# Linear attention and an MLP under one planned order: weight scales from sums of squares, dependencies by up to eight ranges, other virtual times

## The chip, the cores and the metric

The kernel runs on one core of one Trainium2 chip. The core has a matrix engine (PE, with its weight loads listed apart as PEld), a vector engine (DVE), a scalar engine (ACT), a general engine (POOL) and queues that issue DMAs (SP above all). Each engine works through its own instructions in order, and waits where one needs a result of another. The metric is the time of one execution in microseconds. For the kernel before it is the median of three runs.

## The reference

Inputs are `q`, `k`, `v` of shape (8, 8, 576, 64), a projection `w_phi` (64 x 128) and the weights of an MLP, `w_in` (512 x 2048) and `w_out` (2048 x 512). Batch, heads, rows and head width are B, H, S and D.

```python
def phi(x):
    proj = np.einsum('bhsd,df->bhsf', x, w_phi)
    proj = proj - np.max(np.abs(proj), axis=-1, keepdims=True)
    return np.concatenate([np.exp(proj), np.exp(-proj)], axis=-1)
q_p, k_p = (phi(q), phi(k))
kv = np.einsum('bhsf,bhsd->bhfd', k_p, v)
z = np.sum(k_p, axis=2)
num = np.einsum('bhsf,bhfd->bhsd', q_p, kv)
den = np.einsum('bhsf,bhf->bhs', q_p, z)[..., None] + 1e-06
x = (num / den).transpose(0, 2, 1, 3).reshape(B * S, H * D)   # 4608 x 512
h = x @ w_in
out = (h * (1.0 / (1.0 + np.exp(-1.702 * h)))) @ w_out
```

The two weight matrices of the MLP arrive as 8-byte floats: one 128 x 512 block is 512 KB in the profile's list of transfers. The kernel reads their bits as 64-bit integers.

## The kernel before, in words

**Work.** `attention(b)` turns one batch into `x16`, 16-bit high and low parts of the MLP's input, with 512 features on 4 x 128 partitions and the 576 rows of the batch as columns (tile `x`, shape 128 x 2 x 4 x 576). It goes head pair by head pair (`attn_unit`, four to a batch): 512 rows of a pair fill columns 0:512 of one of the four feature groups. The last 64 rows of all heads are done together (`attn_tail`), and `attn_last` (L1086) writes them, when the last pair is through, into columns 512:576 of all 2 x 4 groups at once. The first five units are computed in fp32 (`exact`), the others in split 16-bit pieces.

`moe_chunk` (L1128) does the MLP for a strip of 256 or 384 rows of `x`. For each of 16 blocks `j` of 128 hidden units, 12 matmuls (four feature groups, three products of high and low parts) fill a hidden tile in PSUM (`hps`, two buffers `hb`). ACT takes a tanh (`th`), DVE multiplies (`g`), ACT and DVE split the result in 16-bit parts (`gh`, `gl`), and three matmuls for each 128 rows add it to an output tile (`acc`, three buffers `ab`). The first 512 rows go through the first eight blocks, then through the other eight (`part_` 0 and 1, each in two strips of 256), with the first half's sums kept; the rest of the rows take all 16 blocks in one go.

**Weights.** `load_weights(j)` (L518) reads two blocks of 128 x 512 8-byte floats, one of each matrix, into a staging place: a spare `x` tile (three buffers) or the still unused end of `wbuf`. POOL, ACT and two DVE operations make an fp32 block of each, with the 32-bit words `lo` and `hi` of the raw data as strided views. The first of the two DVE operations leaves magnitudes in place of the `lo` words. Their upper halves, read as bf16, are the moving operand of four matmuls whose stationary operand is a 9-column slice of `pick`, a matrix of zeros with one column of ones. So `wsum` collects, per column of a block, sums of absolute values over the partitions; for `w_in` each block has a row of its own. `weight_scales(k)` (L588) takes the maxima of a half, rounds them down to powers of two and spreads them over the partitions with a matmul; out come `wg`, `sw`, `pg` and, after the second half, `al`. `split_weights(j)` (L609) then scales a block and splits it into 16-bit high and low parts: one operation on ACT, one on DVE. It writes over the block ahead of its source, so the operation on ACT for one block has to wait until DVE has read the block before.

**Order.** The whole order is planned before any instruction is emitted. Each operation is recorded (`Recorder.record`) with a modelled cost and with what it depends on: `touch` (L189) compares the regions that operations read and write in a tile. A region (`V.region`, L77) is a range of partitions and one range of bytes, from the first element to the last; what a strided view leaves out in between counts as touched. `schedule` (L274) goes through the engines like a list scheduler. It takes what could start first, and among what is ready the smaller priority. Operations of a part with `first` for their engine come ahead of all others there. After that goes a virtual time, which `R.part(v0, v1, first)` gives to a stretch of the program. One unit is a chunk of 384 rows of the MLP, whose first strip starts at 0, so that the set-up has negative times. `emit` writes the operations in the planned order. The waits between engines are put in afterwards, from the accesses of the emitted instructions and not from the recorded regions.

The virtual times are at the end of the function (L1183 on): `v_att` for the attention units, `VB` for how long ahead of a batch the maxima of `v` are taken, `WV` for the weights of the two halves (start, step per block, scales) and `SV` for their splits (offset, length). The MLP has first place on DVE and ACT; the split of the first half has it too.

Almost all instructions have one line in the profile, L390, where the recorder emits them. They are told apart by their tiles: `hb<-x,wbuf` is the first product of the MLP, `ab<-wbuf,gh` and `ab<-wbuf,gl` the second, `hb<-...,pick` and `ab<-...,pick` the sums of the weights, `at<-ii,zt` the transposition in `attn_last`, and `wbuf<-wbuf,sw` the splits.

Of the kernel before, what the change touches and what calls it, by code (L numbers as in the profile page):

```python
# [10 lines left out]
F16 = mybir.dt.float16  # L11
BF16 = mybir.dt.bfloat16
I32 = mybir.dt.int32
U32 = mybir.dt.uint32
I64 = mybir.dt.int64
AF = mybir.ActivationFunctionType
# [4 lines left out]
P = 128  # L21
# [25 lines left out]
class V:  # L47
# [29 lines left out]
    def region(self):  # L77
        ap = self.t
        pat = ap.ap
        row = pat[0][0]  # L80
        p0 = ap.start_partition()
        if self.tl.whole:
            return (p0, p0 + pat[0][1], 0, 1 << 20)
# [29 lines left out]
class Recorder:  # L113
# [75 lines left out]
    def touch(self, o, a, write):  # L189
        tl = a.tl  # L190
        self.claim(o, tl)
        p0, p1, b0, b1 = a.region()
        keep = []
        for ent in tl.log:
            (q0, q1, c0, c1), w, d = ent
# [3 lines left out]
            if not (write and d is not o and p0 <= q0 and q1 <= p1 and b0 <= c0 and c1 <= b1):  # L199
                keep.append(ent)  # L200
        keep.append(((p0, p1, b0, b1), write, o))
        tl.log = keep

    @staticmethod
# [189 lines left out]
def attn_moe_kernel(ctx, tc, q, k, v, w_phi, w_in, w_out, out):  # L394
# [12 lines left out]
    NH = 2  # L407
# [59 lines left out]
    nc.vector.tensor_copy(ii[0:D], ident[0:D, 0:D])  # L467
    nc.vector.tensor_copy(ii[D:P], ident[D:P, D:P])

    ones = cp.tile([16, P], F32, name="ones")  # L470
    nc.gpsimd.memset(ones, 1.0)

    wst = static("wst", [P, NF], F32)
    wb = static("wb", [P, 2 * NF], F32)
# [34 lines left out]
        )  # L509
        R.vector.tensor_scalar(dst, dst, 2.0**-50, None, ALU.max)  # L510


    NS = NJ // NH + 1
    pick = cp.tile([P, 2 * NS - 1], BF16, name="pick")
    nc.gpsimd.memset(pick, 0.0)
    nc.gpsimd.memset(pick[:, NS - 1 : NS], 1.0)

    def load_weights(j, wsum, first, last):  # L518
        js = slice(j * P, (j + 1) * P)
        stage = None  # L520
        if WIDE and (j % 4 > 1 or j >= NJ - 4):
            stage = new("x").rearrange("p a c s -> p (a c s)")
        for i, src in (
            (2 * j, w_in[:, js].rearrange("(c p) f -> p c f", p=P)),
            (2 * j + 1, w_out[js, :]),
        ):
            dst = wbuf[:, i + 1]
            if not WIDE:
                if i % 2 == 0:
                    dst = dst.rearrange("p (c f) -> p c f", c=NCT)  # L530
                R.sync.dma_start(dst, src)
                z = new("osb")
                R.scalar.activation(z, wbuf[:, i + 1], AF.Abs)
# [54 lines left out]
    def weight_scales(k, wsum):  # L588

        m = small(1, "sc")[0:NS]  # L590
        m2 = small(NS, "sc")[0:NS]
# [638 lines left out]
    for part_ in range(NH):  # L1230
        js = range(part_ * NJ // NH, (part_ + 1) * NJ // NH)
        v0, dv, v1 = WV[part_]
        wsum = R.tile(ab if part_ else hb, whole=True)[0:NS, 0:P]
        for i, j in enumerate(js):
            R.part(v0 + dv * i, v0 + dv * (i + 1))
            load_weights(j, wsum, j == js[0], j == js[-1])
        R.part(v1, v1)
        weight_scales(part_, wsum)
# [59 lines left out]
```

## Time and profile before

| what | value |
|---|---|
| median of 3 runs | 1095.7 us (1092.83 to 1096.32) |
| the profiled execution | 1094.31 us, of which its span is 1092.5 us |
| mean granted clock of PE | 0.993 |
| PE matmuls | 8941 |
| DMA | 88.59 MB, 81 GB/s on average |

The page lists busy time per engine, and the queries behind it give windows of the span, groups of instructions and the timeline of one engine. A line of the timeline has a start, a duration, the engine, the operation, what it writes and reads (out<-in) and how many of them run on; in brackets stands how long the engine was idle before, and what ended that. The duration of a run of matmuls includes the tail of the last one, so the distance between two starts is the better measure of what a run costs. In a window, the pair of numbers for an engine is its busy time and its count of instructions; PEclk is the share of full clock granted to PE.

### The profile page before, as it was taken

The page shows a single profiled execution, that of the slowest core. Times are in us where ns is not written, and L with a number is a line of the kernel's source. Part 1 is how long each engine was busy: PE and PEld are TensorE (multiplying, and loading weights), DVE is VectorE, ACT ScalarE, POOL GpSimd, SP SyncE. Part 2 cuts the span into 40 slices and gives each one's busy share as a digit, 9 for nine tenths or more (in the row PEclk, how much of TensorE's full clock was granted, in tenths as well). Part 3 has the DMA queues.
Part 4 walks back from the last instruction along what each step waited for, and adds up shares of the span by engine and source line. Part 5 has one row for each costly group of instructions (what it writes and reads, how often), then busy time and mean ns, then how long its engine had stood idle before and what let it go on. Part 6 is the DMA issues. An engine that isn't in the chain of part 4 may idle for free.

```text
span 1092.5 us, 22970 instructions
## 1 busy us (share of the span) xinstructions
PE 1055.1 (97%) x8941; PEld 728.4 (67%) x8941; DVE 866.8 (79%) x1802; ACT 713.4 (65%) x1488; POOL 249.8 (23%) x322
## 2 busy tenths in 40 slices
PE   5996999999999999999999999999999999999997
PEld 3664677668876666578866666678776666577653
DVE  5999999999999997898789987898779766332323
ACT  4677687678787676686667666786567766442422
POOL 6476211241232211301122112111123111100000
PEclk9998999999999999999999999999999999999999
DMA  8853342543253441332234442332224220000101
GB/s 274 271 187 123 94 107 64 107 93 89 59 103 92 117 100 42 69 102 59 49 98 92 118 77 55 68 79 59 59 59 78 36 53 11 11 30 1 30 1 29
DMA packets 177452, 88.59 MB, mean 81 GB/s; under 512 B 143424, under 2 KB 168128, under 8 KB 177088
## 3 DMA queue, kind: packets, MB, share of 16 engines
q1 hardware_dynamic: 177184, 86.87, 32.8%
q8 instruction: 70, 1.15, 0.4%
q10 hardware_dynamic: 160, 0.26, 0.1%
q14 instruction: 38, 0.31, 0.1%
HBM read 54.59 MB, written 9.44 MB: 59 GB/s over the span
## 4 chain that ended last, share of the span: by engine, by line
PE 74%; DVE 14%; ACT 5%; DMA 3%; issue 2%; SPq 1%; POOL 1%; DVEq 0%; ACTq 0%
PE ab L390 29%; PE hb L390 28%; PE at L390 17%; DVE sm L390 2%; DMA xT<-xs 2%; DVE t L390 1%; ACT e L390 1%; DVE gl L390 1%; DVE wbuf L390 1%; DVE g L390 1%; DVE ks L390 1%; SPq L390 1%; DMA tl<-in_v_dram 1%; ACT eh L390 1%; DVE xs L390 1%
## 5 line engine op out<-in xcount | busy, mean ns | idle before, releaser
L390 PE MATMUL hb<-x,wbuf 128*128 128x192 f16 (+3 forms) x3264 | 474.5, 280 | 1.0 <-DVE g L390 0.9
L390 PE MATMUL ab<-wbuf,gh 128*128 128x512 f16 x1152 | 337.0, 380 | 2.2 <-ACT gh L390 2.1
L390 PEld LDWEIGHTS <-wbuf 128*128 128x128 f16 x3264 | 277.4, 98 | 79.2 <-issue 2.2
L390 ACT ACTIVATE th<-hb,usc 128x384 f32<-128x384 f32 (+1 forms) x208 | 116.6, 561 | 130.9 <-PE hb L390 120.0
L390 PE MATMUL ab<-wbuf,gl 128*128 128x512 f16 x576 | 193.1, 380 | 2.6 <-DVE gl L390 2.3
L390 DVE SCALAR_TENSOR_TENSOR g<-th,hb 128x384 f32<-128x384 f32 (+1 forms) x208 | 107.3, 516 | 89.7 <-ACT th L390 87.7
L390 PEld LDWEIGHTS <-gh 128*128 128x128 f16 x1152 | 107.7, 98 | 81.7 <-ACT gh L390 5.8
L390 ACT ACTIVATE gh<-g,al 128x384 f16<-128x384 f32 (+1 forms) x176 | 107.8, 613 | 54.4 <-DVE g L390 53.3
L390 DVE SCALAR_TENSOR_TENSOR gl<-g,al,gh 128x384 f16<-128x384 f32 (+1 forms) x176 | 110.0, 625 | 37.3 <-ACT gh L390 30.2
L390 POOL TENSOR_TENSOR xf<-nf,rc 128x512 f32<-128x512 f32 x28 | 32.7, 1169 | 422.6 <-DVE rc L390 376.2
L390 PE MATMUL at<-ph,xT 128*128 128x128 f16 x976 | 107.1, 219 | 0.1
L390 DVE TENSOR_REDUCE sm<-at 128x4 f32<-128x512 f32 x126 | 85.8, 681 | 19.1 <-PE at L390 18.9
L390 ACT ACTIVATE e<-t 128x512 f32<-128x512 f32 x144 | 89.8, 637 | 10.7 <-DVE t L390 10.5
L390 ACT ACTIVATE e<-at 128x512 f32<-128x512 f32 x144 | 85.9, 604 | 14.8 <-PE at L390 12.7
L390 DVE SCALAR_TENSOR_TENSOR t<-at,ks,sm 128x512 f32<-128x512 f32 x122 | 90.4, 743 | 1.1
L390 PEld LDWEIGHTS <-gl 128*128 128x128 f16 x576 | 54.7, 98 | 52.0 <-DVE gl L390 9.6
L390 PE MATMUL at<-vs,eh 128*128 128x132 f32 x216 | 82.5, 383 | 0.0
L390 DVE TENSOR_TENSOR el<-e,eh 128x512 f16<-128x512 f32 x108 | 74.5, 690 | 9.7 <-ACT eh L390 7.9
L390 DVE TENSOR_TENSOR elb<-e,eh 128x512 bf16<-128x512 f32 x110 | 76.7, 698 | 5.9 <-ACT eh L390 4.9
L390 PE MATMUL at<-kzs,eh 128*128 128x132 f32 x224 | 80.3, 373 | 0.0
L390 PEld LDWEIGHTS <-xT 128*128 128x128 f16 x976 | 70.6, 98 | 14.1 <-issue 0.5
L390 ACT ACTIVATE eh<-t 128x512 fp32r<-128x512 f32 x109 | 69.2, 647 | 0.4 <-DVE t L390 0.3
(204 smaller groups left out, 1898.7 us busy)
## 6 DMA issues: line engine op xcount, KB each, us to landing
vn<-in_v_dram SPq DMA_DIRECT2D x64, 128.0 KB, 2.8
kq<-in_k_dram SPq DMA_DIRECT2D x32, 256.0 KB, 3.1
kq<-in_q_dram SPq DMA_DIRECT2D x32, 256.0 KB, 3.0
tl<-in_v_dram SPq DMA_DIRECT2D x18, 384.0 KB, 3.2
x<-in_moe_w_in_dram SPq DMA_DIRECT2D x10, 512.0 KB, 3.9
x<-in_moe_w_out_dram SPq DMA_DIRECT2D x10, 512.0 KB, 4.6
out_dram<-osb SPq DMA_DIRECT2D x36, 128.0 KB, 2.4
out_dram<-osb SPq DMA_DIRECT2D x16, 256.0 KB, 2.6
```

The lines of the kernel that those rows point to most:

```text
L390: f(*[g(a) for a in args], **{k: g(a) for k, a in kw.items()})
```

## The change

It has three parts.

**Ranges.** `region` returns up to eight byte ranges where a view has that many pieces, each at least 32 elements apart from the next; `touch` compares all ranges of both.

```diff
-        lo = ap.offset - p0 * row
-        hi = lo + 1 + sum(s * (n - 1) for s, n in pat[1:])
-        return (p0, p0 + pat[0][1], lo * b, hi * b)
+        los, rest = [ap.offset - p0 * row], list(pat[1:])
+        while rest and len(los) * rest[0][1] <= 8:
+            inner = 1 + sum(s * (n - 1) for s, n in rest[1:])
+            if rest[0][0] < inner + 32:
+                break
+            los = [x + rest[0][0] * k for x in los for k in range(rest[0][1])]
+            rest = rest[1:]
+        n = 1 + sum(s * (n - 1) for s, n in rest)
+        return (p0, p0 + pat[0][1], tuple((x * b, (x + n) * b) for x in los))
...
-            hit = q0 < p1 and p0 < q1 and c0 < b1 and b0 < c1
+            hit = q0 < p1 and p0 < q1 and any(c0 < b1 and b0 < c1 for b0, b1 in rs for c0, c1 in cs)
```

**Sums of squares.** The stationary operand of the weights' matmuls is now the block's own 128 columns, the same as the moving one, so each adds a 128 x 128 product of the block with itself, whose diagonal holds the sums of squares. `w_in` and `w_out` have one such square each in `wsq`. The operands are the upper halves of the finished fp32 weights in `wbuf`, no longer of words in the staging tile. ACT is recorded ahead of POOL. `weight_scales` takes the maxima of both squares, transposes them, takes the maxima again, halves the exponent with an integer shift (a square root, rounded to a power of two) and spreads the two results with a second matmul.

```diff
-                R.gpsimd.tensor_scalar(y, hi.bitcast(F32), 2.0**-112, None, ALU.mult)
-                z = lo
-                R.scalar.activation(z, lo.bitcast(U32), AF.Copy, scale=0.9375 * 2.0**-29)
+                R.scalar.activation(lo, lo.bitcast(U32), AF.Copy, scale=0.9375 * 2.0**-29)
+                R.gpsimd.tensor_scalar(y, hi.bitcast(F32), 2.0**-112, None, ALU.mult)
                 R.vector.scalar_tensor_tensor(
-                    z, y.bitcast(I32), 3, z, ALU.logical_shift_left, ALU.bitwise_or
+                    y.bitcast(I32), y.bitcast(I32), 3, lo, ALU.logical_shift_left, ALU.bitwise_or
                 )
                 R.vector.scalar_tensor_tensor(
-                    dst.bitcast(I32), hi, -(2**31), z, ALU.bitwise_and, ALU.bitwise_or
+                    y.bitcast(I32), hi, -(2**31), y.bitcast(I32), ALU.bitwise_and, ALU.bitwise_or
                 )
-                z = raw.bitcast(BF16).rearrange("p (n w) -> p n w", w=4)[:, :, 1]
-            r = NS - 1 if i % 2 else j % (NS - 1)
+            z = wbuf[:, i + 1].bitcast(BF16).rearrange("p (n w) -> p n w", w=2)[:, :, 1]
             for c in range(NCT):
+                zc = z[:, c * P : (c + 1) * P]
                 R.tensor.matmul(
-                    wsum,
-                    pick[:, NS - 1 - r : 2 * NS - 1 - r],
-                    z[:, c * P : (c + 1) * P],
+                    wsq[:, i % 2],
+                    zc,
+                    zc,
...
-        R.vector.tensor_reduce(m, wsum, AX.X, ALU.max)
-        pow2(m, m)
-        R.vector.tensor_scalar(m2, ident[0:NS, 0:NS], m, None, ALU.mult)
+        R.vector.tensor_reduce(m, wsq, AX.X, ALU.max)
         tp = psa()
-        R.tensor.matmul(tp[:, 0:NS], ones[0:NS], m2, start=True, stop=True)
-        R.vector.tensor_reduce(wg[:, k, 0:1], tp[:, 0 : NS - 1], AX.X, ALU.max)
-        R.vector.tensor_copy(wg[:, k, 1:2], tp[:, NS - 1 : NS])
+        R.tensor.transpose(tp[0:2, 0:P], m, ident)
+        R.vector.tensor_reduce(m1, tp[0:2, 0:P], AX.X, ALU.max)
+        R.vector.tensor_scalar(
+            m1.bitcast(I32), m1.bitcast(I32), 1, 0x7F800000,
+            ALU.logical_shift_right, ALU.bitwise_and,
+        )
+        R.vector.tensor_scalar(m1, m1, 2.0**64, 2.0**-50, ALU.mult, ALU.max)
+        R.vector.tensor_scalar(m2, wone, m1, None, ALU.mult)
+        R.tensor.matmul(tp[:, P : P + 2], ones[0:2], m2, start=True, stop=True)
+        R.vector.tensor_copy(wg[:, k], tp[:, P : P + 2])
```

**Virtual times.** First place on DVE and ACT goes from the split of the first half to that of the second.

```diff
-    VB = 0.532
-    V1 = (-1.793, 0.5)
-    WV = ((-9.335, 0.3, -7.2), (-7.049, 0.246, -5.399))
-    SV = ((-0.438, 1.101), (0.0, 0.212))
+    VB = 0.882
+    V1 = (-1.39, 0.435)
+    WV = ((-9.335, 0.3, -7.395), (-6.76, 0.267, -5.253))
+    SV = ((-0.955, 1.101), (0.223, 0.212))
...
-            return -10.175 + 1.0 * i
+            return -10.175 + 0.983 * i
...
-        return 0.776 + (i - 8) * 0.362
+        return 0.519 + (i - 8) * 0.366
...
-                R.part(u, u + (0.321 if b else 0.1))
+                R.part(u, u + (0.266 if b else 0.1))
...
-            R.part(w, w + (0.537 if b else 0.2))
+            R.part(w, w + (0.517 if b else 0.2))
...
-        R.part(v2, v2 + SV[part_][1], () if part_ else ("vector", "scalar"))
+        R.part(v2, v2 + SV[part_][1], ("vector", "scalar") if part_ else ())
```

More of the change, by code (lines that the diff above doesn't have):

```diff
@@ L13 @@
 I32 = mybir.dt.int32
+I16 = mybir.dt.int16
 U32 = mybir.dt.uint32
@@ L191, in touch @@
         self.claim(o, tl)
-        p0, p1, b0, b1 = a.region()
+        p0, p1, rs = a.region()
         keep = []
         for ent in tl.log:
-            (q0, q1, c0, c1), w, d = ent
-            hit = q0 < p1 and p0 < q1 and c0 < b1 and b0 < c1
+            (q0, q1, cs), w, d = ent
+            hit = q0 < p1 and p0 < q1 and any(c0 < b1 and b0 < c1 for b0, b1 in rs for c0, c1 in cs)
             if hit and (w or write) and d is not o:
                 o.deps[d] = True
-            if not (write and d is not o and p0 <= q0 and q1 <= p1 and b0 <= c0 and c1 <= b1):
+            over = write and d is not o and p0 <= q0 and q1 <= p1
+            if not (over and all(any(b0 <= c0 and c1 <= b1 for b0, b1 in rs) for c0, c1 in cs)):
                 keep.append(ent)
-        keep.append(((p0, p1, b0, b1), write, o))
+        keep.append(((p0, p1, rs), write, o))
         tl.log = keep
@@ L468, in attn_moe_kernel @@
     nc.vector.tensor_copy(ii[D:P], ident[D:P, D:P])
-    ones = cp.tile([16, P], F32, name="ones")
+    ones = cp.tile([2, P], F32, name="ones")
     nc.gpsimd.memset(ones, 1.0)
+    wone = cp.tile([2, 2], F32, name="wone")
+    nc.vector.tensor_scalar(wone[:, 0:1], ident[0:2, 0:1], 16.0, None, ALU.mult)
+    nc.vector.tensor_copy(wone[:, 1:2], ident[0:2, 1:2])
     wst = static("wst", [P, NF], F32)
@@ L510, in pow2, with load_weights @@
         R.vector.tensor_scalar(dst, dst, 2.0**-50, None, ALU.max)
[L513 to L518, printed above, removed]
+    def load_weights(j, wsq, first, last):
         js = slice(j * P, (j + 1) * P)
@@ L531, in load_weights @@
                 R.sync.dma_start(dst, src)
-                z = new("osb")
-                R.scalar.activation(z, wbuf[:, i + 1], AF.Abs)
             else:
@@ L586, in allmax, with weight_scales @@
         R.vector.tensor_copy(dst, tp[:, P : P + 1])
-    def weight_scales(k, wsum):
-        m = small(1, "sc")[0:NS]
-        m2 = small(NS, "sc")[0:NS]
-        R.vector.tensor_reduce(m, wsum, AX.X, ALU.max)
-        pow2(m, m)
-        R.vector.tensor_scalar(m2, ident[0:NS, 0:NS], m, None, ALU.mult)
-        tp = psa()
-        R.tensor.matmul(tp[:, 0:NS], ones[0:NS], m2, start=True, stop=True)
-        R.vector.tensor_reduce(wg[:, k, 0:1], tp[:, 0 : NS - 1], AX.X, ALU.max)
-        R.vector.tensor_copy(wg[:, k, 1:2], tp[:, NS - 1 : NS])
+    def weight_scales(k, wsq):
+        m = small(2, "sc")
+        m1 = small(1, "sc")[0:2]
+        m2 = small(2, "sc")[0:2]
+        R.vector.tensor_reduce(m, wsq, AX.X, ALU.max)
+        tp = psa()
+        R.tensor.transpose(tp[0:2, 0:P], m, ident)
[8 more added lines that the diff above has]
+        R.vector.tensor_copy(wg[:, k], tp[:, P : P + 2])
         R.vector.reciprocal(sw[:, k], wg[:, k])
@@ L1232, in attn_moe_kernel @@
         v0, dv, v1 = WV[part_]
-        wsum = R.tile(ab if part_ else hb, whole=True)[0:NS, 0:P]
+        wsq = R.tile(ab if part_ else hb, whole=True)[:, 0 : 2 * P]
+        wsq = wsq.rearrange("p (t f) -> p t f", t=2)
         for i, j in enumerate(js):
             R.part(v0 + dv * i, v0 + dv * (i + 1))
-            load_weights(j, wsum, j == js[0], j == js[-1])
+            load_weights(j, wsq, j == js[0], j == js[-1])
         R.part(v1, v1)
-        weight_scales(part_, wsum)
+        weight_scales(part_, wsq)
         v2 = v1 + SV[part_][0]
-        R.part(v2, v2 + SV[part_][1], () if part_ else ("vector", "scalar"))
+        R.part(v2, v2 + SV[part_][1], ("vector", "scalar") if part_ else ())
         for j in js:
```

2 lines of the change are left out of this document (1 added, 1 removed).

## The prediction

> **What bounds the kernel now.** I read the page's totals first, then the busy time of each engine by windows, then the timeline of PE where PE is idle.
>
> ```profile
> span 1092.5 us, 22970 instructions
> PE 1055.1 (97%) x8941; PEld 728.4 (67%) x8941; DVE 866.8 (79%) x1802; ACT 713.4 (65%) x1488; POOL 249.8 (23%) x322
> ...
> 50.00:100.00 50.00, 46.41 (x276) 30.29 (x276) 48.18 (x98) 38.81 (x78) 33.38 (x23) 1.00 0.53 167
> 100.00:150.00 50.00, 42.80 (x280) 28.36 (x281) 47.09 (x94) 34.87 (x70) 18.18 (x16) 0.86 0.36 95
> 150.00:200.00 50.00, 49.07 (x474) 37.55 (x472) 49.40 (x106) 42.40 (x96) 10.99 (x13) 1.00 0.36 86
> 200.00:250.00 50.00, 47.91 (x484) 35.64 (x483) 49.43 (x120) 33.45 (x77) 13.50 (x17) 1.00 0.51 110
> 250.00:300.00 50.00, 49.61 (x639) 40.88 (x636) 49.62 (x120) 40.06 (x92) 9.38 (x14) 1.00 0.27 61
> ```
>
> The columns are span, then busy time of PE, weight loads, DVE, ACT and POOL, then PE's granted clock. PE is busy for 1055.1 of 1092.5 us, so it sets the time: only its idle time, its slow clock and its own work can be saved. From 150 to 300 it is idle for at most 2.1 us in 50. Between 100 and 150 it is idle for 7.2 us, and the clock is 0.86. DVE meanwhile is 94 to 99% busy all the way to 300, which the rivals below come back to. The hole itself, in PE's timeline:
>
> ```profile
> 89.19 0.27 PE L390 MATMUL hb<-x,wbuf 128*128 128x256 f16 x1
> ...
> 97.63 0.23 PE L390 MATMUL at<-kzb,eqtlb 128*128 128x132 bf16 x1
> 100.74 1.09 PE L390 MATMUL at<-ident,xf 128*128 128x128 f32 x4 [2.88 <-DVE xf L390]
> 102.44 0.62 PE L390 MATMUL ab<-x,pick 128*9 128x128 bf16 x4 [0.62 <-DVE x L390]
> 105.39 0.62 PE L390 MATMUL ab<-x,pick 128*9 128x128 bf16 x4 [2.32 <-DVE x L390]
> 106.24 0.40 PE L390 MATMUL at<-ii,zt 128*128 128x64 f16 x4 [0.23 <-ACT zt L390]
> 108.12 0.62 PE L390 MATMUL ab<-x,pick 128*9 128x128 bf16 x4 [1.48 <-DVE x L390]
> ...
> 110.84 0.62 PE L390 MATMUL ab<-x,pick 128*9 128x128 bf16 x4 [1.77 <-DVE x L390]
> 111.40 4.75 PE L390 MATMUL hb<-x,wbuf 128*128 128x256 f16 x31
> 115.99 1.03 PE L390 MATMUL ab<-wbuf,gh 128*128 128x512 f16 x4
> ```
>
> From 97.86 to 111.40 PE does a few small groups and waits 2.88 + 0.62 + 2.32 + 0.23 + 1.48 + 1.77 = **9.30 us**. Then the MLP (`hb<-x,wbuf`) breaks loose with 31 matmuls. One matmul of it stands alone at 89.19, and one more of the next hidden tile a little later. They say why it waits. The first matmul of a hidden tile reads columns 0:256 of row 0 of `x`; the second reads row 0 of the low half. `attn_last` writes only columns 512:576 of all eight rows, but L77 records that write as one range from the first to the last byte. Row 0's first 256 columns lie ahead of that range, everything after lies in it. There are two `hb` buffers, so two hidden tiles each issue one matmul and then stand behind `attn_last` in the planned order:
>
> ```profile
> 102.31 0.57 ACT L390 CAST x<-at 128x512 f16<-128x512 f32 x1
> 109.81 0.57 ACT L390 CAST x<-at 128x512 f16<-128x512 f32 x1
> ...
> 104.06 0.68 DVE L390 TENSOR_TENSOR x<-at,x 128x512 f16<-128x512 f32 x1
> ```
>
> What the MLP's first 512 columns need is the last head pair's `x`, complete at 104.06 + 0.68 = 104.74. `attn_last`'s copy ends only at 110.38.
>
> **The change, part by part.** *(a) Ranges.* With up to eight ranges the write becomes its eight true pieces, and the planner may start the MLP at 104.74. The price of one such matmul at full clock comes from a long run:
>
> ```profile
> 149.93 3.45 PE L390 MATMUL hb<-x,wbuf 128*128 128x256 f16 x29
> 153.26 1.04 PE L390 MATMUL ab<-wbuf,gh 128*128 128x512 f16 x4
> ```
>
> That is 3.33 / 29 = 0.115 us. Three of the four row groups of `x` are there earlier, so 9 of 12 matmuls of two hidden tiles, less the two that run already, fit into the wait: 16 x 0.115 = 1.8 us. What stood between 104.74 and 111.40 (three `pick` groups at 0.62 and two groups of `ii,zt` at 0.40, 2.66 us as shown) comes later, at 1.5 us by the prices of (c). Gain: 6.66 - 1.5 + 1.8 = **7.0**. Idle time left before 104.74: 6.88 - 1.09 - 0.2 - 1.8 = 3.8. Bounds: nothing (second rival) to the whole 9.3.
>
> *(b) Clock.* The burst at 111.40 takes 4.59 / 31 = 0.148 us each against 0.115: 1.0 us lost. With 3.8 us still idle I take half, **0.5** (0 to 1.0).
>
> *(c) Sums on PE.* 128 matmuls in 32 groups of four turn from a 9-column to a 128-column stationary operand; `pick` is no longer loaded.
>
> ```profile
> 119.97 0.62 PE L390 MATMUL ab<-x,pick 128*9 128x128 bf16 x4
> 120.52 0.50 PE L390 MATMUL hb<-x,wbuf 128*128 128x256 f16 x3
> 120.86 0.67 PE L390 MATMUL at<-ph,xT 128*128 128x128 f16 x9
> 121.36 0.61 PE L390 MATMUL at<-ident,kq 128*128 128x128 f32 x4
> ...
> 124.25 0.62 PE L390 MATMUL ab<-x,pick 128*9 128x128 bf16 x4
> ...
> L390 PEld LDWEIGHTS <-xT 128*128 128x128 f16 x976 | 70.6, 98 | 14.1 <-issue 0.5
> L390 PEld LDWEIGHTS at<-kzs,eh 128*128 128x128 f32 x224 | 42.6, 191 | 2.9 <-issue 0.5 <-POOL vt L390 0.4 <-POOL kzs L390 0.3
> L390 PEld LDWEIGHTS <-pick 128*9 128x9 bf16 x128 | 11.4, 99 | 12.8 <-issue 11.2 <-DMA wbuf<-in_moe_w_out_dram 0.2
> ```
>
> A `pick` group holds PE for 0.55 us. Nine full-width matmuls of 128 columns go in 0.50, so four take 0.22: 0.33 saved per group. The last of the 32 groups is that at 124.25, and it is the fourth after 111.40, where PE is the bound: 1.3. The earlier ones stand beside a DVE that has 1.8 us idle in 50:100, so the PE time they free is mostly worth nothing; I take 1.0. Together **2.3**. The new operand is read in steps of 4 bytes, which no row shows. If it loaded like fp32 (191 ns, plus 56 for the matmul) a group would cost 1.0, 0.45 more than now, for at most eight groups where PE is the bound: -3.6. The other end is eight groups saved and all 1.8: +4.4. I stay by the nearest row, 16-bit and 128 wide.
>
> The Trainium skill ("TensorE: Matmul & The Clock Gate", LDWEIGHTS) speaks against this edit: a load takes its columns divided by 1.2, in ns, so 9 columns would take 8 ns and 128 columns 107, and the new matmuls would cost more, not less; an estimate by it is 0.1 us more per matmul and a term of -3.2 for eight groups. The trace has 99 ns for 9 columns and 98 for 128, so here the row decides against the rule.
>
> *(d) Unpacking.* Per block still one ACT, one POOL and two DVE operations; the second DVE operation is now ahead of the matmul (0.68 later), and the staging buffer comes free without PE. ACT goes ahead of POOL in the plan. Off the path while PE has the MLP to do: 0.
>
> *(e) Scales.* `weight_scales` has one trip to PE and back more, and about 0.3 us more on DVE.
>
> ```profile
> 75.14 0.30 DVE L390 TENSOR_SCALAR sc<-ident,sc 9x9 f32<-9x9 f32 x1
> 79.39 0.39 PE L390 MATMUL at<-sc,ones 9*128 9x9 f32 x2
> 80.53 0.15 DVE L390 TENSOR_REDUCE wg<-at 128x1 f32<-128x8 f32 x1
> ...
> 83.49 0.74 DVE L390 SCALAR_TENSOR_TENSOR wbuf<-wbuf,sw 128x512 f16<-128x512 f32 x1
> ...
> 119.69 0.74 DVE L390 SCALAR_TENSOR_TENSOR wbuf<-wbuf,sw 128x512 f16<-128x512 f32 x1
> ```
>
> A trip takes 80.53 - 75.44 = 5.1 us, since PE serves its queue in order. The 16 split steps of the first half (83.49 to 119.69, 2.41 us each) then end at 125.5. The MLP would want the last one at 104.74 + 7 x 2.7 = 123.6 (12 x 0.115 and 6 x 0.22 per hidden tile). So it is 1.9 late, with attention matmuls of batch 1 to fill in (120.86 above): **-1.0** (0 to -5).
>
> *(f) Virtual times.* The second half's weights move from -7.05 to -6.76, behind the last head pair of batch 0 (about -7.2). The high half of that pair's `x` is ready at 102.88 and the low half starts on DVE at 104.06, so 1.2 us could be won there, but the split steps in front of it stay in front. Batch 1's attention moves from -1.79 to -1.39, with nothing planned in between; batch 2's comes 0.26 earlier. PE's idle time from 150 to 300 is 0.93 + 2.09 + 0.39 = 3.4, so a new order can win or lose about 3: **0** (-3 to +3, and up to 1.2 for `x`).
>
> Sum: 7.0 + 0.5 + 2.3 - 1.0 = 8.8, from the profiled execution's own 1094.3 (span 1092.5 and 1.8 around it) 1085.5. The median shown is 1.4 higher, which would give 1086.9; I forecast **1086**.
>
> **The rivals.** *DVE is the real bound to 245.* The next chunk of the MLP needs batch 1's attention, and that is finished only just in time:
>
> ```profile
> 241.25 0.28 PE L390 MATMUL at<-ii,zt 128*128 128x64 f16 x4
> ...
> 245.88 1.40 DVE L390 SCALAR_TENSOR_TENSOR osb<-ab,osf,x 128x512 f32<-128x512 f32 x2
> ```
>
> DVE's idle time from 100 to 250 is 2.91 + 0.60 + 0.57 = 4.1. If all that it does before 245 has to come before 245, the gain comes back as waits there, all but some 2 of those 4.1: 1092. Against it: some of DVE's work there, batch 2's maxima of v and its first features, isn't needed by 245 and can slip. Chance 0.15.
>
> *Starved by the split: slower.* The first half's split loses its first place on DVE and ACT, and the MLP's four operations per hidden tile (th and gh on ACT, g and gl on DVE) keep theirs.
>
> ```profile
> L390 DVE SCALAR_TENSOR_TENSOR gl<-g,gh 128x256 f16<-128x256 f32 x32 | 15.9, 498 | 0.4 <-ACT gh L390 0.2
> ```
>
> With all four at 0.5 us ahead of every step, 2.41 becomes 4.4. About half of the 16 steps are done when the MLP starts; eight more from 105.6 end at 105.6 + 35.2 + 0.7 = 141.5, 18 after 123.6. PE, in order, waits for it: of that 1.0 is in the sum already, 1085.5 + 17 = 1102. It decides, against no change, from a step of about 3.4, and is slower than before by what can be told (0.3%, below) from about 4.0. For it: the steps are a chain of ACT and DVE in turn. Against: attention is there to fill in. Chance 0.10.
>
> *The wide operand loads slowly*, (c) at -3.6: 1091. Chance 0.06.
>
> *The wait is real*: the order changes, but the waits in the program are as coarse as the plan's. Then only (c) and (e) are left, 1093. Against it speak two engines that write interleaved pieces of the one `vs` buffer at the same time:
>
> ```profile
> 301.25 0.61 POOL L390 CAST vs<-v 128x512 fp32r<-128x512 f16 x1 [0.24 <-ACT v L390]
> 301.61 0.80 DVE L390 SCALAR_TENSOR_TENSOR vs<-vn,iv,v 128x512 fp32r<-128x512 f32 x1
> ```
>
> Chance 0.04. *Better*: the hole closes wholly, (a) 9.3, (b) 1.0, (c) 4.4 and 2 of (f): 1077. Chance 0.08.
>
> **How the numbers follow.** The forecast has 0.57, and by itself 1080 to 1091. The sums of the bounds run from 1075 (all at their best) to 1099 (all but (a) at their worst); leaving out the ends, 1076 to 1097 holds all but the starved case and the tails. A measurement of this kernel can tell about 0.3%, 3.3 us, from no change, so faster is below 1092.4 and slower above 1099.0. Faster: 0.55 of the forecast, 0.08, 0.04 of the slow load, 0.07 of the DVE case, 0.01: 0.75. Slower: the starved case and 0.01 of the DVE case: 0.11. The rest, 0.14, is the same.
>
> **What would show it.** (a): nine matmuls on each of the first two `hb` tiles well before the last head pair's `x`, the rest before the copy of `attn_last`, and PE's idle time in 95:115 under 5 us. (b): a clock above 0.86 in 100:150. (c): groups of four in about 0.25 us and no issue wait ahead of their loads. (e): the last split step near 125. PE waits on `wbuf` between 115 and 140 would show the starved case; PE waits on batch 1's attention between 200 and 245 the DVE case. I am wrong if the hole is gone and the end has not moved.

## The result, and the profile after

| kernel | median (lowest to highest), us | ratio to before, 95% interval |
|---|---|---|
| before | 1095.7 (1092.83 to 1096.32) | 1 |
| after | 1088.6 (1087.29 to 1090.62) | 0.9938 (0.9927 to 0.995) |

The change takes 0.6% off, 7 us where 9.7 were forecast. The profiled execution of after took 1088.60, its span 1086.8. Its line numbers are nine higher: the recorder's L390 is now L399. The totals, and the same windows as before (span, then busy time and count of PE, weight loads, DVE, ACT and POOL, then PE's granted clock):

```profile
span 1086.8 us, 22956 instructions
PE 1045.9 (96%) x8943; PEld 724.9 (67%) x8943; DVE 868.8 (80%) x1804; ACT 714.8 (66%) x1488; POOL 252.7 (23%) x320
...
50.00:100.00 50.00, 43.65 (x297) 29.70 (x297) 48.89 (x97) 39.43 (x79) 36.51 (x26) 0.99 0.55 171
100.00:150.00 50.00, 44.90 (x301) 30.80 (x302) 48.74 (x103) 37.57 (x76) 13.61 (x13) 0.87 0.30 82
150.00:200.00 50.00, 49.08 (x470) 37.13 (x469) 50.00 (x115) 40.73 (x92) 11.72 (x13) 1.00 0.46 98
200.00:250.00 50.00, 49.61 (x535) 38.52 (x534) 49.74 (x113) 38.44 (x90) 18.03 (x22) 1.00 0.33 81
```

PE has 9.2 us less work (1055.1 to 1045.9), but its idle time has grown from 37.4 to 40.9, so that the span falls by 5.7 only. The hole is still there: 5.1 us idle from 100 to 150, where it was 7.2, and the clock in this window is 0.87 after 0.86. The 2.1 us less are not a smaller hole, since in after the hole begins ahead of 100: from 50 to 150 PE is idle for 11.5 us, before for 10.8. DVE has 1.26 + 0 + 0.26 = 1.5 us idle left from 100 to 250, where it had 4.1. The hole itself, in PE's timeline:

```profile
84.73 1.48 PE L399 MATMUL ab<-wbuf 128*128 128x128 bf16 x23
86.05 0.27 PE L399 MATMUL hb<-x,wbuf 128*128 128x256 f16 x1
...
87.94 0.38 PE L399 MATMUL hb<-x,wbuf 128*128 128x256 f16 x2
...
88.23 0.72 PE L399 MATMUL hb<-x,wbuf 128*128 128x256 f16 x5
...
101.37 0.61 PE L399 MATMUL ab<-wbuf 128*128 128x128 bf16 x4 [4.55 <-DVE wbuf L399]
102.21 1.12 PE L399 MATMUL at<-ident,xf 128*128 128x128 f32 x4 [0.23 <-DVE xf L399]
105.25 0.61 PE L399 MATMUL ab<-wbuf 128*128 128x128 bf16 x4 [1.93 <-DVE wbuf L399]
...
107.56 1.01 PE L399 MATMUL hb<-x,wbuf 128*128 128x256 f16 x4 [1.06 <-DVE x L399]
...
109.57 2.29 PE L399 MATMUL hb<-x,wbuf 128*128 128x256 f16 x10 [0.36 <-DVE g L399]
111.65 1.51 PE L399 MATMUL ab<-wbuf,gh 128*128 128x512 f16 x4
...
114.51 0.39 PE L399 MATMUL ab<-wbuf 128*128 128x128 bf16 x4
114.74 0.38 PE L399 MATMUL ab<-wbuf,gl 128*128 128x512 f16 x1
```

`ab<-wbuf` without a second input are the sums of squares. From 86.05 on the MLP's matmuls (`hb<-x,wbuf`) run early, 18 of them before 97 where two had. But the waits are 4.55 + 0.23 + 1.93 + 1.06 + 0.36 = 8.1 us, little less than the 9.30 of before. The two longest end with a block that DVE has unpacked for the sums, and the matmuls that need the low half of the last head pair's `x`, the part that DVE writes, start at 107.56. DVE's timeline says why:

```profile
103.33 0.84 DVE L399 SCALAR_TENSOR_TENSOR xs<-tl,ks,xs 128x256 f16<-128x256 f32 x1
104.09 1.10 DVE L399 SCALAR_TENSOR_TENSOR wbuf<-x,wbuf 128x512 int32<-128x512 int32 x1
105.12 1.12 DVE L399 SCALAR_TENSOR_TENSOR wbuf<-wbuf,x 128x512 int32<-128x512 int32 x1
106.17 0.74 DVE L399 SCALAR_TENSOR_TENSOR wbuf<-wbuf,sw 128x512 f16<-128x512 f32 x1
106.83 0.68 DVE L399 TENSOR_TENSOR x<-at,x 128x512 f16<-128x512 f32 x1
```

That `x` is complete at 107.51, before at 104.74. In the new order two unpacking operations and a split (`wbuf<-wbuf,sw`) stand in DVE's queue right ahead of it.

### The profile page after: what moved, and what is told of

The parts are those of the page before. It is cut to its first block, busy times and chain, and to the rows that moved or that the text cites. A ratio compares the mean times of both kernels' runs of the same rounds, so it can differ in the third digit from the quotient of the medians.

```text
span 1086.8 us, 22956 instructions
## 1 busy us (share of the span) xinstructions
PE 1045.9 (96%) x8943; PEld 724.9 (67%) x8943; DVE 868.8 (80%) x1804; ACT 714.8 (66%) x1488; POOL 252.7 (23%) x320
## 4 chain that ended last, share of the span: by engine, by line
PE 66%; DVE 22%; ACT 5%; issue 4%; DMA 2%; SPq 1%; POOL 0%; DVEq 0%; ACTq 0%; POOLq 0%
PE ab L399 27%; PE hb L399 26%; PE at L399 13%; DVE wbuf L399 3%; DVE sm L399 3%; DVE t L399 2%; DVE ks L399 2%; DVE gl L399 2%; DVE el L399 1%; DVE g L399 1%; DVE elb L399 1%; DVE xs L399 1%; ACT e L399 1%; DMA xT<-xs 1%; DVE sc L399 1%
## 5 line engine op out<-in xcount | busy, mean ns | idle before, releaser
L399 PE MATMUL hb<-x,wbuf 128*128 128x192 f16 (+3 forms) x3264 | 476.9, 280 | 3.3 <-DVE g L399 2.1
L399 PEld LDWEIGHTS <-wbuf 128*128 128x128 f16 (+1 forms) x3392 | 286.6, 98 | 91.6 <-DVE wbuf L399 10.9
L399 PE MATMUL ab<-wbuf,gh 128*128 128x512 f16 x1152 | 338.8, 380 | 0.6 <-ACT gh L399 0.5
L399 ACT ACTIVATE th<-hb,usc 128x384 f32<-128x384 f32 (+1 forms) x208 | 116.1, 558 | 139.3 <-PE hb L399 136.7
L399 PE MATMUL ab<-wbuf,gl 128*128 128x512 f16 x576 | 194.3, 380 | 2.4 <-DVE gl L399 2.4
L399 DVE SCALAR_TENSOR_TENSOR g<-th,hb 128x384 f32<-128x384 f32 (+1 forms) x208 | 107.6, 518 | 93.0 <-ACT th L399 90.4
L399 PEld LDWEIGHTS <-gh 128*128 128x128 f16 x1152 | 108.0, 98 | 79.6 <-ACT gh L399 2.1
L399 DVE SCALAR_TENSOR_TENSOR gl<-g,al,gh 128x384 f16<-128x384 f32 (+1 forms) x176 | 109.4, 622 | 41.4 <-ACT gh L399 32.8
L399 ACT ACTIVATE gh<-g,al 128x384 f16<-128x384 f32 (+1 forms) x176 | 107.1, 609 | 53.5 <-DVE g L399 52.8
L399 POOL TENSOR_TENSOR xf<-nf,rc 128x512 f32<-128x512 f32 x28 | 34.9, 1246 | 422.9 <-DVE rc L399 361.5
L399 PE MATMUL at<-ph,xT 128*128 128x128 f16 x976 | 103.3, 219 | 0.1
L399 DVE TENSOR_REDUCE sm<-at 128x4 f32<-128x512 f32 x126 | 86.2, 684 | 17.6 <-PE at L399 17.3
L399 ACT ACTIVATE e<-t 128x512 f32<-128x512 f32 x144 | 89.1, 634 | 11.6 <-DVE t L399 11.3
L399 ACT ACTIVATE e<-at 128x512 f32<-128x512 f32 x144 | 85.6, 601 | 14.6 <-PE at L399 13.4
L399 DVE SCALAR_TENSOR_TENSOR t<-at,ks,sm 128x512 f32<-128x512 f32 x122 | 90.7, 745 | 1.1
L399 PEld LDWEIGHTS <-gl 128*128 128x128 f16 x576 | 54.9, 98 | 51.7 <-DVE gl L399 9.3
L399 DVE TENSOR_TENSOR el<-e,eh 128x512 f16<-128x512 f32 x108 | 75.2, 696 | 13.7 <-ACT eh L399 12.3
L399 DVE TENSOR_TENSOR elb<-e,eh 128x512 bf16<-128x512 f32 x110 | 78.2, 711 | 5.8 <-ACT eh L399 4.4
L399 PE MATMUL at<-vs,eh 128*128 128x132 f32 x216 | 82.1, 380 | 0.0
L399 PE MATMUL at<-kzs,eh 128*128 128x132 f32 x224 | 79.4, 372 | 1.3 <-DVE kzs L399 1.3
L399 PEld LDWEIGHTS <-xT 128*128 128x128 f16 x976 | 69.7, 98 | 13.2 <-issue 1.3
L399 ACT ACTIVATE eh<-t 128x512 fp32r<-128x512 f32 x109 | 68.1, 639 | 0.9 <-DVE t L399 0.9
```

The lines of the kernel that those rows point to most:

```text
L399: f(*[g(a) for a in args], **{k: g(a) for k, a in kw.items()})
```

## The experiments

Names with b_ are edits of the kernel before, with a_ of the kernel after. All were timed against runs of before on the same chip, whose medians were 1095.85, 1095.15 and 1094.4 in the three groups. Beside the times I use one number that can be followed through the span. **Lost time** at a moment t is t less the useful matmul work begun until then, where a matmul counts with the median distance between two starts of its shape in the trace of before (16-bit: 0.056 us for 128 columns, 0.109 for 256, 0.216 for 512) and the sums over the weights count nothing. Before has lost some 50 us by 130. The table gives each kernel's difference to before in lost time, worked out from PE's timelines; negative is ahead. One profiled execution may lie up to 3 us off its kernel's median, and its trace as far off in the table: after and a_jitter issue the same matmuls in the same order up to 369 us, yet differ by 2.1 us at 130. Most of that arises between 43.0 and 46.4, which a_jitter ran at a clock of 0.50 and after at 1.00.

| kernel | last pair's `x` ready | at 97 | 112 | 130 | 200 | 300 | 500 | end |
|---|---|---|---|---|---|---|---|---|
| before | 104.74 | | | | | | | |
| after | 107.51 | -2.5 | -3.2 | -5.3 | -4.9 | -5.7 | -9.2 | -5.3 |
| b_ranges | 110.36 | +1.5 | -1.8 | -0.4 | +1.2 | -0.5 | -2.6 | -2.1 |
| b_squares | 104.39 | -0.8 | -3.0 | -5.1 | -4.9 | -3.7 | -3.2 | -3.3 |
| b_times | 105.13 | +0.4 | +0.1 | +0.3 | +4.6 | +5.7 | +5.1 | +6.7 |
| a_no_ranges | 104.27 | -0.8 | -3.1 | -5.4 | -3.4 | -3.6 | -5.1 | -2.7 |
| a_no_squares | 109.90 | +0.8 | -2.0 | -1.0 | +1.1 | +0.1 | -2.4 | -0.6 |
| a_no_times | 107.52 | -2.5 | -3.6 | -6.1 | -6.4 | -4.9 | -6.8 | -5.3 |
| a_last_pair_first | 102.36 | -2.5 | -5.4 | -8.6 | -4.2 | -4.9 | -5.3 | -1.1 |
| b_wide_pick | 103.23 | -1.0 | -2.2 | -3.9 | -3.5 | -4.7 | -6.9 | -7.5 |
| b_wide_ranges | 101.41 | -2.7 | -6.4 | -8.2 | -7.8 | -5.8 | -6.4 | -6.1 |
| b_step4 | 111.52 | +1.8 | +0.4 | +2.9 | +3.1 | +4.9 | +4.4 | +2.2 |
| b_jitter | 104.61 | -0.1 | -0.1 | -0.2 | 0.0 | +0.4 | -1.0 | +1.5 |
| a_jitter | 109.50 | -1.9 | -2.2 | -3.2 | -2.6 | -4.4 | -7.3 | -6.0 |

**One part alone, in the kernel before.** Only the ranges:

```diff
-        return (p0, p0 + pat[0][1], lo * b, hi * b)
+        return (p0, p0 + pat[0][1], tuple((x * b, (x + n) * b) for x in los))
```

> The kernel before with the ranges alone (region and touch of after; sums by pick and virtual times as before). Theory A, the prediction: the ranges let the MLP start before attn_last, worth about 7.5 us (terms a and b): ratio 0.993, the hole before the first run of the second product at 116 us shrinks by 4 or more. Theory B, drawn from the profile after (idle time of PE did not shrink, 37.4 to 40.9 us, but its busy time fell by 9.2): the hole is DVE's and stays; the ranges only move a few matmuls ahead of it: ratio 0.997 to 1.000.

Measured 1091.6, 0.9962 (0.9949 to 0.9975). PE's timeline of it in the hole:

```profile
102.86 0.62 PE L398 MATMUL ab<-x,pick 128*9 128x128 bf16 x4 [0.21 <-DVE x L398]
105.62 0.62 PE L398 MATMUL ab<-x,pick 128*9 128x128 bf16 x4 [2.14 <-DVE x L398]
107.89 1.12 PE L398 MATMUL at<-ident,xf 128*128 128x128 f32 x4 [1.66 <-DVE xf L398]
...
111.36 0.40 PE L398 MATMUL at<-ii,zt 128*128 128x64 f16 x4 [1.08 <-ACT zt L398]
```

The transposition of `xf`, from which the last pair's `x` is made, comes at 107.89, where it came at 100.74. So the ranges let 16 MLP matmuls go ahead of 97, but they also turned DVE's queue over and made the last `x` 5.6 us late. By 130 nothing is left of the gain (-0.4). What the median shows comes later, after 200, and is of the size of the accidents below.

Only the sums of squares:

```diff
-                    pick[:, NS - 1 - r : 2 * NS - 1 - r],
-                    z[:, c * P : (c + 1) * P],
+                    zc,
+                    zc,
```

> The kernel before with the sums of squares alone (load_weights and weight_scales of after). Theory A: terms c and e together +1.3 us of gain at most: ratio 0.999. Theory B: the 32 narrow groups each held PE for 0.55 us, and PE time saved anywhere after 30 us comes out at the end: ratio 0.992 to 0.995.

Measured 1089.62, 0.9947 (0.9936 to 0.9959), most of the whole change. PE's work falls by 9.4 us, in after by 9.2, and `x` stays in its place:

```profile
PE 1045.7 (96%) x8943; PEld 726.2 (67%) x8943; DVE 867.5 (80%) x1804; ACT 714.4 (66%) x1488; POOL 243.0 (22%) x320
...
96.00:112.00 16.00, 8.01 (x66) 6.42 (x64) 15.94 (x26) 9.85 (x20) 13.48 (x12) 0.68 0.71 206
112.00:150.00 38.00, 37.04 (x257) 25.52 (x255) 36.81 (x84) 27.48 (x58) 7.79 (x9) 1.00 0.32 85
```

All of it is won by 130 (-5.1).

Only the virtual times:

```diff
-    WV = ((-9.335, 0.3, -7.2), (-7.049, 0.246, -5.399))
-    SV = ((-0.438, 1.101), (0.0, 0.212))
+    WV = ((-9.335, 0.3, -7.395), (-6.76, 0.267, -5.253))
+    SV = ((-0.955, 1.101), (0.223, 0.212))
...
-        return 0.776 + (i - 8) * 0.362
+        return 0.519 + (i - 8) * 0.366
```

> The kernel before with the virtual times alone. Theory A and B alike: nothing on balance, ratio 0.997 to 1.003. A third theory, that the times carry the gain, has 0.994 here.

Measured 1100.49, 1.0043 (1.003 to 1.0056): by themselves the new times cost 4.6 us. Up to 130 it has lost only 0.3 more than before; 4.3 follow by 200, most of them at one place, as PE's timeline and a window behind it show:

```profile
182.03 0.33 PE L390 MATMUL at<-kzs,eh 128*128 128x132 f32 x1 [1.88 <-POOL kzs L390]
...
183.00:186.40 3.40, 3.40 (x24) 2.37 (x22) 1.49 (x5) 0.93 (x2) 0.55 (x1) 0.50 0.48 136
```

PE waits 1.88 us for one operand that POOL makes, and then runs at half clock for 3.4 us, which loses 1.7 more.

**One part undone, in the kernel after.** Each is the reverse of one of the three edits above, and so the corners of the change are complete.

> The kernel after with one range per operand again (squares and times stay). The parts alone gave 0.9962 (ranges), 0.9947 (squares) and 1.0043 (times). If they add up, this gives 0.998 to 0.999. If the ranges only pay where the hole is filled anyway, it stays at 0.994 to 0.996.

> The kernel after with the sums by pick again (ranges and times stay). If the parts add up: 1.000. If the squares are what carries the change, as the PE time lost up to 130 us says (5.4 us less with the squares alone, 0.4 less with the ranges alone), the loss up to 130 us comes back to within 1 us of the kernel before.

> The kernel after with the virtual times of before (ranges and squares stay). If the parts add up: 0.990, faster than after. If the new times fit the new dependencies and costs and only hurt the old ones: 0.994 to 0.998, not faster than after.

| ranges | squares | times | kernel | median, us | ratio |
|---|---|---|---|---|---|
| yes | no | no | b_ranges | 1091.6 | 0.9962 (0.9949 to 0.9975) |
| no | yes | no | b_squares | 1089.62 | 0.9947 (0.9936 to 0.9959) |
| no | no | yes | b_times | 1100.49 | 1.0043 (1.003 to 1.0056) |
| no | yes | yes | a_no_ranges | 1091.4 | 0.9968 (0.9956 to 0.998) |
| yes | no | yes | a_no_squares | 1094.45 | 0.9992 (0.9983 to 1.0001) |
| yes | yes | no | a_no_times | 1090.7 | 0.996 (0.9946 to 0.9973) |
| yes | yes | yes | after | 1088.6 | 0.9938 (0.9927 to 0.995) |

Each part can be read in four pairs of rows, as thousandths of the time. Squares: -5.3, -7.5, -0.2, -5.4. Ranges: -3.8, -5.1, +1.3, -3.0. Times: +4.3, +3.0, +2.1, -2.2. The squares are the only part that never costs anything, though in one pair they give nothing that can be told; ranges and times change sign with what stands beside them. The parts don't add up: ranges and squares without the times give -4.0, not -9.1.

The same four pairs at 130 us, from the table of lost time, are far steadier. Squares: -5.1, -5.7, -5.7, -4.3. Ranges: -0.4, -1.3, -1.0, +0.1. Times: +0.3, -0.6, -0.3, +0.8. Up to there the squares carry the gain, and neither of the other two goes beyond the 2 us by which two traces of one order differ.

**A plan differing in nothing that matters.** How much of that is accident of the order? The slope of the attention times was moved by 0.001 in both kernels:

```diff
-        return 0.776 + (i - 8) * 0.362
+        return 0.776 + (i - 8) * 0.363
```

> The kernel before with 0.363 in place of 0.362 as step of the virtual times from batch 2 on: nothing of the work or its costs changes, the first 300 us or so keep their order, later pieces change places. If the order there is worth little: ratio 0.999 to 1.001. If differences of 2 to 4 us between the variants after 130 us are an accident of the order, it moves by as much, 0.997 to 1.003.

> The kernel after with 0.365 in place of 0.366, the same test on it. Robust: 0.993 to 0.995. Accident: anything from 0.991 to 0.998.

The second has 0.365 in place of 0.366. Measured 1.0016 (1.0007 to 1.0025) for before, and 1084.91, 0.992 (0.9907 to 0.9932), for after. An edit that means nothing moves the time by 1.7 us one way and by some 2 to 4 the other (2 by the ratios, 4 by the medians; the intervals of after and a_jitter just overlap). PE's order is the same up to 318 us in before and b_jitter. The averages of the four pairs above are -2.7 thousandths for the ranges and +1.8 for the times, and each scatters by 6: neither can be told from such accidents. The squares' average of -4.6 scatters by 7; at the end of the span it stands out, if not by much, and what makes it sure are the four pairs at 130.

**What a group of four costs.** Two things change with the squares: the stationary operand has 128 columns, not 9, and the moving one is read in steps of 4 bytes, not of 8. First the width alone; the sums of one column stay in their row, the other rows are not used. The planner's model sees the width too (`schedule` adds 95 ns, L361, where the class of the stationary operand changes: up to 32 rows or columns, up to 64, or more), so the order changes with it:

```diff
-    pick = cp.tile([P, 2 * NS - 1], BF16, name="pick")
+    pick = cp.tile([P, NS - 1 + P], BF16, name="pick")
...
-                    pick[:, NS - 1 - r : 2 * NS - 1 - r],
+                    pick[:, NS - 1 - r : NS - 1 - r + P],
```

> The kernel before with pick widened from 9 to 128 columns (zeros but for one column), so that only the width of the stationary operand changes, nothing of the sums' data flow. If the narrow operand is what costs, a group of four takes about 0.25 us in place of 0.55, PE's busy time falls by 8 to 10 us and, by theory B, the ratio is 0.993 to 0.996; by theory A 0.998. If the 8-byte steps of the moving operand cost, the groups stay at 0.55 and the ratio at 1.000.

Measured 1086.31, 0.9914 (0.9901 to 0.9927), faster than before and, by intervals that only touch, than after. Its loads in the table of groups, and two places of PE's timeline:

```profile
L390 PEld LDWEIGHTS <-pick 128*128 128x128 bf16 x128 | 13.9, 112 | 3.3 <-issue 1.9
...
85.90 2.01 PE L390 MATMUL ab<-wbuf,pick 128*128 128x128 bf16 x16
87.74 0.64 PE L390 MATMUL ab<-x,pick 128*128 128x128 bf16 x4
88.20 0.29 PE L390 MATMUL hb<-x,wbuf 128*128 128x256 f16 x1
```

Sixteen matmuls take 1.84, 0.115 each, and a group 0.46, where 9 columns took 0.55 (prediction, 119.97 to 120.52). The loads' 11.2 us of issue wait are down to 1.9.

Then the step alone: 9 columns, with the values of the finished weights in steps of 4 bytes. The sums are then of signed values, not of magnitudes, and the matmuls wait for the second DVE operation, as in after.

```diff
-                z = raw.bitcast(BF16).rearrange("p (n w) -> p n w", w=4)[:, :, 1]
+                z = dst.bitcast(BF16).rearrange("p (n w) -> p n w", w=2)[:, :, 1]
```

> The kernel before, its sums by the 9-column pick, but over the upper halves of the finished weights in wbuf (signed, in steps of 4 bytes, as the squares read them) in place of the magnitudes in the staging tile (steps of 8 bytes): the scales come from sums of signed values. If the step of the moving operand sets the pace inside a group, its matmuls follow each other at 0.06 us in place of 0.115 and a group takes about 0.33 us where it took 0.55; what is left above 0.23 is the narrow operand. If the width sets it, groups stay at 0.55.

Measured 1094.61, 1.0004 (0.9995 to 1.0013). A group's place in PE's timeline, and the loads in its table of groups:

```profile
119.54 0.40 PE L390 MATMUL ab<-wbuf,pick 128*9 128x128 bf16 x4
119.87 0.39 PE L390 MATMUL ab<-wbuf,gh 128*128 128x512 f16 x1
...
L390 PEld LDWEIGHTS <-pick 128*9 128x9 bf16 x128 | 7.8, 88 | 12.3 <-issue 10.8
```

The group takes 0.33, so 32 of them free 32 x 0.22 = 7 us of PE, and none of it reaches the end: `x` of the last pair is 6.8 us late in this order, and by 130 the kernel is 2.9 behind. Part of that is no matter of the order: the trace has a clock of 0.50 from 22.7 to 26.1 and from 43.1 to 46.5, where before has 1.00, and the kernel is 1.8 behind at 97 already. It fits that PE time is worth something only where PE is the bound; this run alone doesn't show it.

**Does the late `x` hold the ranges' gain back?** In after, the last pair of batch 0 gets first place on DVE and ACT:

```diff
-            R.part(w, w + (0.517 if b else 0.2))
+            R.part(w, w + (0.517 if b else 0.2), ("vector", "scalar") if b == 0 and hp == NHP - 1 else ())
```

> The kernel after with first place on DVE and ACT for the last head pair of batch 0, whose x was finished at 107.5 us though its numerators stood at 97.8, behind weight unpacking and splits in DVE's queue. If that queue keeps the hole open, x is there by 103 and the first run of the second product, 111.65 after, comes 3 to 5 us earlier: ratio 0.990. If DVE's total work up to then sets it, what is moved ahead delays the splits and the ratio stays at 0.994.

Measured 1091.87, 0.9968 (0.9955 to 0.998), slower than after by some 3 us. Yet `x` is ready at 102.36 and the hole closes as meant, by 8.6 us at 130 where after has 5.3. Then it is lost again. PE's busy time in it, by windows, and its longer waits after 150, from the timeline:

```profile
150.00:200.00 50.00, 47.39 (x439) 34.61 (x437) 48.82 (x114) 37.65 (x85) 9.93 (x13) 1.00 0.48 100
200.00:250.00 50.00, 47.54 (x514) 36.41 (x512) 49.15 (x110) 39.76 (x91) 13.70 (x17) 1.00 0.37 85
...
151.72 2.23 PE L399 MATMUL hb<-x,wbuf 128*128 128x256 f16 x19 [1.12 <-DVE g L399]
156.72 0.59 PE L399 MATMUL ab<-wbuf,gh 128*128 128x512 f16 x2 [0.88 <-ACT x L399]
...
229.45 1.05 PE L399 MATMUL at<-ph,xT 128*128 128x128 f16 x16 [0.72 <-DVE nf L399]
```

PE is idle for 5.1 us between 150 and 250, in after for 1.3. That the load of DVE takes back what the hole gives is not shown: of 4.3 us of waits there, 2.3 end with DVE, 1.3 with ACT and 0.7 with a DMA, and in after DVE is busier still (99.7% against 98%). The other 4 us or so, behind 500, are all lost between 600 and 613, at one wait and the half clock that follows it:

```profile
608.47 0.81 PE L399 MATMUL at<-ident,t 128*128 128x128 f32 x4 [2.22 <-DVE t L399]
...
608.83:612.25 3.42, 3.42 (x18) 2.14 (x17) 3.30 (x9) 2.23 (x5) 0.00 (x0) 0.50 0.12 41
```

The wait and half of the 3.4 us make 3.9. After has a wait of 1.80 at the same operand, and keeps its clock.

The same question in the kernel before, wide `pick` and ranges together (the two diffs above):

> The kernel before with the 128-column pick and with the ranges. Alone they gave 0.9914 and 0.9962; if they add up, 0.988, faster than both kernels. If the wide pick's gain after 130 us (3.6 of its 7.5) is an accident of its order, the new order loses it again: 0.992 to 0.996.

Measured 1088.45, 0.9947 (0.9935 to 0.996). DVE's timeline has the last `x` early:

```profile
100.74 0.67 DVE L398 TENSOR_TENSOR x<-at,x 128x512 f16<-128x512 f32 x1
```

By 130 it is 8.2 ahead, the wide `pick` alone 3.9: with `x` early the ranges give 4.3 there. By 300 the difference is 1.1, and at the end it is on the other side.

## Why the prediction was right, and where it was wrong

The sign, the forecast case and the range held. The distribution over the terms did not, and the sign of being wrong that was named ("the hole is gone and the end has not moved") came the other way round: the hole stayed, and the end moved.

*(a) Ranges, 7.0 forecast: the step that failed.* The mechanism is there. The false dependence is what kept the MLP back: 16 to 18 of its matmuls run before 97 in every kernel with ranges, and two in every kernel without. The working then held the last pair's `x` at 104.74 and counted from there. But DVE's queue is planned anew with the rest, and with the ranges that `x` came at 107.5 to 110.4 in five kernels of seven; in all four pairs that differ by the ranges alone they made it 3.1 to 5.6 us later. So by 130 the ranges gave 1.3 us at the most in these pairs, and -0.1 in the step from a_no_ranges to after, not 7.0. Where `x` came early, they gave 4.3 by 130 (b_wide_ranges), and first place for the last pair made after 3.3 better there. Why the planner puts the `x` later stays open; the ranges are not the only edit that does (b_step4, 111.52). PE's idle time in 95:115, forecast under 5 us, is 8.5, before 9.3.

*(b) Clock, 0.5 forecast.* Nothing. Half clock lasts as long as before, as the windows of before and of after show:

```profile
100.40:113.70 13.30, 6.54 (x39) 4.40 (x40) 13.09 (x19) 6.93 (x13) 10.74 (x8) 0.50 0.39 121
```

```profile
99.20:112.40 13.20, 7.46 (x42) 5.08 (x43) 13.20 (x24) 8.19 (x16) 11.10 (x9) 0.50 0.28 86
```

Its length does not follow from the hole alone. From 45 to 105 us a_no_times issues the same matmuls as after, at the same times to 0.03 us, with the same waits of 4.55 and 1.93, yet its half clock lasts from 101.0 to 111.3, 3.4 us less. So some of the differences of about 1 us between kernels at 130 are accidents of the clock.

*(c) Sums on PE, 2.3 forecast: right in its direction, too small.* A group takes 0.23 (114.51 to 114.74) after 0.55, the 0.33 that I took, and the matmul ahead of a 9-column group used to stretch by 0.10 too: 0.42. By 130 the squares are worth 5.1 alone and 4.3 beside the others (a_no_squares to after). Of that, 4 x 0.42 = 1.7 comes from the four groups behind 112. The 0.10 ahead of a group is what the sum lacked, though the kernel's own planner charges 95 ns for such a change (L361). Half clock is shorter in b_squares, though in after it is not:

```profile
99.50:109.30 9.80, 4.67 (x36) 3.79 (x37) 9.74 (x14) 6.01 (x11) 8.86 (x9) 0.50 0.57 140
```

The load of 128 columns went as the row for the same width said. The Trainium skill ("TensorE: Matmul & The Clock Gate", LDWEIGHTS), by which 9 columns would load in 8 ns and 128 in 107, fits the 128 columns of the widened `pick`, which took 112 ns. For 9 columns it is contradicted a second time, by 88 ns in b_step4 after 99 in before, and the kernel with the wider operand is the faster one.

*(d) Unpacking and (e) scales, 0 and -1.0.* The first and last DVE operation of the chain in before, then in after, with the last split of the first half:

```profile
72.67 0.27 DVE L390 TENSOR_REDUCE sc<-hb 9x1 f32<-9x128 f32 x1
...
80.61 0.14 DVE L390 COPY wg<-at 128x1 f32<-128x1 f32 x1
```

```profile
73.84 0.41 DVE L399 TENSOR_REDUCE sc<-hb 128x2 f32<-128x256 f32 x1
...
80.59 0.10 DVE L399 COPY wg<-at 128x2 f32<-128x2 f32 x1
...
122.67 0.75 DVE L399 SCALAR_TENSOR_TENSOR wbuf<-wbuf,sw 128x512 f16<-128x512 f32 x1
```

With its second trip to PE the chain takes 6.85 us, where it took 8.08 with one. The two trips, from DVE's result to DVE's next step, take 2.8 us (74.25 to 77.04) and 2.1 (78.46 to 80.59): 5.1 us was no fixed price of a trip, but that of the queue that happened to stand on PE. The last split ends at 123.4, forecast 125.5, wanted 123.6. So (e) cost nothing that can be seen, and the rival "starved by the split" did not occur.

*(f) Times, 0 (-3 to +3).* In after they are worth some 2 us (intervals that overlap), in the other three pairs they cost 2 to 5. The bounds were about right; that this term has the size of an accident could have been said, and not only for (f): every change of a dependence turns the order over.

*The rivals.* **DVE as the bound to 245** did not come true in after. Its sign was to be PE's waits between 200 and 245; PE is idle for 0.39 us from 200 to 250, and the lead of 5.3 us at 130 is 5.7 at 300. A bound further off is possible: by 130 the kernels of the table with squares or the wide `pick` are ahead by anything from 3.2 to 8.6 us; at 300 all of them are ahead by 3.6 to 5.8. That would fit a bound that leaves some 5 us, not 2, but the waits in a_last_pair_first don't point to DVE alone, and no run tests it.

*Luck.* Too much was put on the ranges (7.0, where they gave 1.3 at the most by 130) and too little on the squares (2.3, where they gave 4.3 to 5.7). These two errors cancelled in part, and of the 7 us measured 5.3 are there by 130; the rest came where the accidents are. That the total fell near the forecast is luck.

Two kernels lie below after, with intervals that touch or overlap its own: b_wide_pick at 0.9914 (0.9901 to 0.9927) and a_jitter at 0.992 (0.9907 to 0.9932). The intervals of b_squares, b_wide_ranges and a_no_times overlap that of after from above. Of b_wide_pick's 7.5 us, 3.9 are there by 130; the rest comes after 200 and is gone when the ranges are added, so I count it to the accidents. Which single decisions of the plan make them stays open but for the waits shown in b_times and a_last_pair_first.

## What to carry to other kernels

Where one planner orders everything, a removed dependence is not a removed wait: all queues are dealt anew, so ask of each operand that the freed work still needs where it will stand in the new order, and don't take its old time as given. Move a meaningless constant a little, in both kernels, before a gain of under half a per cent is put down to an edit. And count what a group of small matmuls costs by the distance from its first start to the next work's start, with the operand's step and width in view, not by its columns alone.

## What the runs showed of the hardware

A group of four matmuls with 128 moving columns of 16 bits, at full clock:

| stationary columns | step of the moving operand | first start to next start | kernel |
|---|---|---|---|
| 9 | 8 bytes | 0.55 | before, 119.97 to 120.52 |
| 128 | 8 bytes | 0.46 | b_wide_pick, 87.74 to 88.20 |
| 9 | 4 bytes | 0.33 | b_step4, 119.54 to 119.87 |
| 128 | 4 bytes | 0.23 | after, 114.51 to 114.74 |

The step of 8 bytes doubles a matmul's time: 0.115 each (1.84 / 16 in b_wide_pick) against 0.057 (84.73 to 86.05 in after, 1.32 / 23). Nine columns add 0.1 us at the end of a group, whatever the step, and, by the median over the distances in the timelines, 0.1 ahead of it; 128 add neither. What the array does at such a change of width no trace shows; the 95 ns that the kernel's planner charges for it (L361) are of that size.

The Trainium skill ("Advanced Engine Details and Errata", SBUF Cachelines) says of SBUF's lines of 16 bytes that at least two hits on a line are needed to absorb the access latency. Two accesses to a line were not enough here: a step of 8 bytes makes just two, and runs at half; a step of 4 makes four, and runs at full.

Some short waits of PE were followed by 3.4 us at half clock, and some were not. One of 1.88 us in b_times was, and one of 2.22 in a_last_pair_first; waits of 2.71 (up to 238.51) and 2.08 (up to 565.76) in a_no_times and of 1.80 (up to 604.90) in after were not. Half clock in the hole lasted 13.65 us in before and after, and 10.24 in b_squares, a_no_ranges, a_no_times, a_last_pair_first and b_wide_ranges, which is 3.4 less. after and a_no_times have the same PE timeline from 45 to 105: from 99 to 101, where PE is idle in both, the clock is 0.50 in one and 1.00 in the other.
